# Scan adds and segment sums put on GpSimd, first state reloads issued from GpSimd's queue, half of Wo loaded behind the first attention outputs

## The chip, the cores and the metric

The kernel runs on one core of one Trainium2 chip. The metric is the device time of one execution in microseconds (us). A time below is the median of several executions, with the lowest and highest in brackets.

The engines are called PE (TensorE, the matmuls), VectorE (DVE in the profile), ScalarE (ACT), GpSimd (POOL) and SyncE (SP, which here only issues DMAs). Each works through its own instructions in order.

## The reference, cut to what matters

Two layers read inputs of 2048 x 1024 each, and their results are put side by side.

```python
# A: a state space layer, 1024 complex states
h = Lam_bar[None, :] * h + Bu[:, t, :]                     # for each of 2048 steps
y = 2.0 * einsum('blp,dp->bld', hseq, Cmat).real + x * Dskip
# B: attention over 64 segments of 32 tokens with 8 memory rows, 32 heads of 128
h = concatenate([mem, xs], axis=1)                          # for each segment
q, k, v = h @ Wq, h @ Wk, h @ Wv
o = softmax(mask(q @ k.T * scale)) @ v                      # by head
o = einsum('bhte,hed->btd', o, Wo); mem = o[:, :8]; outs.append(o[:, 8:])
```

## The kernel before

The kernel runs through four stages.

1. For each of 8 blocks of 128 states and each of 4 blocks of 512 steps, PE makes 16 products of 128x512 for A (L225) and, between them, 32 products for B's values (L364). VectorE turns A's products, runs two scans, and turns them back. The states go to DRAM.
2. The states are reloaded and multiplied by C (L284). Products of B's mean with Wo (L404 below, "the Wo products") stand between.
3. Attention.
4. Its outputs are reloaded and multiplied by Wo (L597).

```python
# stage 1, one block of states (pc) and one block of steps (tb)
V.tensor_tensor(wr[:], ur[:], c_, ALU.mult)      # ur, ui lie in PSUM, c_ and s_ in SBUF
V.tensor_tensor(ta[:], ui[:], s_, ALU.mult)
V.tensor_tensor(wr[:], wr[:], ta[:], ALU.add)                  # L231
V.tensor_tensor(wi[:], ui[:], c_, ALU.mult)
V.tensor_tensor(ta[:], ur[:], s_, ALU.mult)
V.tensor_tensor(wi[:], wi[:], ta[:], ALU.subtract)             # L234
V.tensor_tensor_scan(wr[:], rb, wr[:], ..., ALU.mult, ALU.add) # L237
V.tensor_tensor_scan(wi[:], rb, wi[:], ..., ALU.mult, ALU.add) # L238
...                                               # 2 casts on ScalarE, 6 bf16 operations on VectorE
k.SP.dma_start(self.hs[tb][:, pc, :, :], h[:])                 # L258, store of the states

# B's transposed input, 5 loads within the first block of states; each is followed by its sums
k.SP.dma_start_transpose(self.xe[:, :, c:c + n], self.x[0][t:t + n, :])
k.V.tensor_reduce(self.xsum[...], self.xe[...].rearrange("p c (s n) -> p c s n", n=SEG), AX.X, ALU.add)

# stage 2
for tb in range(NB):
    for q in range(4):                            # 0.5 MB each
        k.SP.dma_start(hl[q][:], self.hs[tb][:, 2 * q:2 * q + 2, :, :])
    if dB is None:
        k.SP.dma_start(dB[:], self.Dskip...)      # L271
    for tt in range(4):
        k.SP.dma_start(xn[:], self.x[0][t0:t0 + 128, :])       # L275
        G.tensor_tensor(xd[:], xn[:], dB[:], ALU.mult)         # L277, the skip product
        for half in range(2):
            ...                                   # 16 matmuls into py, one of two PSUM tiles (L284)
            V.tensor_tensor(ot[:, hs], py[:], xd[:, hs], ALU.add)  # L286, frees py
```

When the sums of all five loads are there, VectorE makes the segment means `b_xbar`. PE multiplies them by Wv once for each block of states (L381) and transposes the result (L386). The attention masks and a few constants are built on GpSimd, out of about 60 small operations which the scheduler places in the first block of states.

## Time and profile before

| what | value |
|---|---|
| time | 1345.31 us (1342.99 to 1346.76, 4 runs) |
| PE busy | 1288.2 of 1344.6 us in the profiled run |
| VectorE / GpSimd busy in 120 to 360 us | 209.6 / 0 of 240 us, with PE at 238.8 |
| waits of PE over 4 us | 8.3, 7.6, 7.1, 5.5, 4.8, 4.5 us |

The first view is the page's 40 slices of the span: each digit is the busy share of one slice in tenths, for PE and for GpSimd.

```profile
PE   6898999999979999999999999999999969999998
...
POOL 5000000000012221222222222222223220000000
```

PE is full but for the first slices and the slice near 1100 us (the 6 late in its row). A dip at 390 us hides in a slice of 7. GpSimd has nothing to do in stage 1 after the first slice. That is the spare time which the change wants to use.

The second view is the list of waits of PE: what it waited for, us in total, times, and the longest.

```profile
PE psP L597 <- DMA b_ol<-b_os_90: 8.3, 1, 8.3
PE psO L284 <- DMA a_hl_3523<-a_hs_70: 7.6, 1, 7.6
...
PE psR L386 <- ACT b_vst L62: 5.2, 2, 4.5
PE psP L364 <- DMA b_xe<-in_B_x_dram: 4.8, 1, 4.8
```

The first line is the tail of attention, the second the reload of the states, the third (4.5 of its 5.2 us) a transpose at 114 us, the fourth the fourth load of B's input at 47 us. (It is called "block 3" below, as the count starts at 0.)

In VectorE's timeline (start, duration, engine, line, operation), the first add of the second pair, and the scan that needs it:

```profile
36.93 0.68 DVE L231 TENSOR_TENSOR a_wr<-a_wr,a_ta 128x512 f32<-128x512 f32 x1
...
38.73 1.27 DVE L237 TENSOR_TENSOR_SCAN a_wr<-a_rr,a_nx,a_wr 128x512 f32<-128x512 f32 x1
```

The pair runs at 37 to 41 us, each add in 0.68 us. In SyncE's timeline, the load of B's block 3 is issued before the second store of states:

```profile
44.74 4.92 SPq L338 DMA_TRANSPOSE b_xe<-in_B_x_dram  x1
...
57.83 0.45 SPq L258 DMA_DIRECT2D a_hs_71<-a_h  x1
```

SyncE's timeline at the reload shows 1 MB of Wv issued just before the first states:

```profile
383.05 0.54 SPq L351 DMA_DIRECT2D b_wv<-in_B_Wv_dram  x1
383.64 0.61 SPq L268 DMA_DIRECT2D a_hl_3523<-a_hs_70  x1
...
385.94 0.43 SPq L271 DMA_DIRECT2D a_dB<-in_A_Dskip_dram  x1
```

### The profile page before, as it was taken

What the parts mean: (1) busy time and instruction counts of PE and PEld (TensorE: products, weight loads), DVE (VectorE), ACT (ScalarE), POOL (GpSimd) and SP (SyncE); (2) the same over time, 40 slices, a digit from 0 to 9 for tenths busy, and PEclk for the clock granted to TensorE, in tenths of its full rate; (3) what the DMA queues carried; (4) which work ended last, traced back from release to release, by engine and by line L of the source; (5) the groups of instructions that cost most, each with busy time, mean ns of one, the idle gap of its engine ahead of it and who ended that gap; (6) DMA issues with size and microseconds to landing.
All of it is one profiled execution on the core that took longest, in us unless ns stands there. A gap on an engine that the chain in (4) does not pass through costs nothing. (4 is left out here: it accounts for less than half of the span.)

```text
span 1344.6 us, 19373 instructions
## 1 busy us (share of the span) xinstructions
PE 1288.2 (96%) x7456; PEld 658.4 (49%) x7522; DVE 672.0 (50%) x1490; ACT 434.3 (32%) x1145; POOL 206.0 (15%) x283
## 2 busy tenths in 40 slices
PE   6898999999979999999999999999999969999998
PEld 2343444444434445555555555555555534444443
DVE  6899988888831223455555555555555520001000
ACT  2234333443310000454544545445545530001000
POOL 5000000000012221222222222222223220000000
PEclk9899999999989999999999999999999979999999
DMA  9983423332369726434343433333333082403000
GB/s 225 251 196 118 112 90 104 118 117 71 102 231 326 252 67 203 112 97 130 97 130 97 130 97 114 107 89 90 89 95 89 11 268 85 141 16 125 17 16 26
DMA packets 218873, 163.12 MB, mean 121 GB/s; under 512 B 74944, under 2 KB 198448, under 8 KB 218776
## 3 DMA queue, kind: packets, MB, share of 16 engines
q1 hardware_dynamic: 218200, 161.33, 41.4%
q8 instruction: 61, 1.00, 0.3%
q0 software_dynamic: 512, 0.47, 0.1%
q14 instruction: 36, 0.29, 0.1%
q10 hardware_dynamic: 64, 0.02, 0.0%
HBM read 95.72 MB, written 49.30 MB: 108 GB/s over the span
## 5 line engine op out<-in xcount | busy, mean ns | idle before, releaser
L364 PE MATMUL psP<-b_wv,b_xe 128*128 128x512 bf16 x996 | 226.6, 381 | 7.1 <-DMA b_xe<-in_B_x_dram 4.8
L509 ACT ACTIVATE b_e<-psS 99x396 bf16<-99x396 f32 x176 | 88.2, 501 | 338.9 <-PE psS L506 336.5
L512 POOL TENSOR_TENSOR b_m<-b_e,maskB 99x396 bf16<-99x396 bf16 x160 | 139.4, 871 | 355.3 <-ACT b_e L509 355.3
L532 DVE TENSOR_TENSOR b_ot<-psO,b_r 128x384 bf16<-128x384 f32 x176 | 98.1, 558 | 189.4 <-ACT b_r L526 168.7
L364 PEld LDWEIGHTS <-b_xe 128*128 128x128 bf16 x1024 | 100.4, 98 | 127.6 <-DMA b_xe<-in_B_x_dram 6.4
L597 PEld LDWEIGHTS <-b_ol 128*128 128x128 bf16 x896 | 88.0, 98 | 115.5 <-DMA b_ol<-b_os_90 8.1
L62 ACT ACTIVATE b_vst<-psP 128x512 bf16<-128x512 f32 x128 | 75.0, 588 | 142.2 <-PE psP L364 126.6
L64 DVE CAST b_ost<-psP 128x512 bf16<-128x512 f32 x16 | 11.1, 692 | 202.8 <-PE psP L597 202.8
L597 PE MATMUL psP<-t_4361,b_ol 128*128 128x512 bf16 x438 | 101.0, 385 | 8.7 <-DMA b_ol<-b_os_90 8.3
L597 PE MATMUL psP<-wo_11767,b_ol 128*128 128x512 bf16 x438 | 98.8, 379 | 0.5
L526 ACT ACTIVATE b_r<-b_ln 128x396 f32<-128x396 f32 x176 | 94.0, 534 | 5.4
L525 ACT ACTIVATE b_ln<-psR 128x396 f32<-128x396 f32 x176 | 86.9, 494 | 0.0
L62 ACT ACTIVATE b_ost<-psP 128x512 bf16<-128x512 f32 x16 | 9.6, 597 | 220.7 <-PE psP L597 207.4
L286 DVE TENSOR_TENSOR a_ot<-psO,a_xd 128x512 bf16<-128x512 f32 x32 | 22.1, 692 | 109.5 <-PE psO L284 89.4
L64 DVE CAST b_k_4366<-psP 128x480 bf16<-128x480 f32 (+2 forms) x96 | 48.8, 529 | 32.7 <-PE psP L482 32.2
L530 PE MATMUL psO<-b_m,b_v 99*128 99x99 bf16 x704 | 61.4, 209 | 1.8 <-DMA b_v<-b_vx_74 1.8
L521 PE MATMUL psR<-b_m,ones 99*128 99x396 bf16 x176 | 59.0, 335 | 3.1 <-POOL b_m L512 2.3
L277 POOL TENSOR_TENSOR a_xd<-a_xn_3533,a_dB 128x1024 f32<-128x1024 bf16 x1 | 2.1, 2117 | 374.2 <-DMA a_xn_3533<-in_A_x_dram 374.2
L64 DVE CAST b_k_4374<-psP 128x480 bf16<-128x480 f32 (+2 forms) x96 | 48.7, 528 | 21.2 <-PE psP L482 21.2
L530 PEld LDWEIGHTS <-b_v 99*128 99x128 bf16 x704 | 50.5, 98 | 15.3 <-DMA b_v<-b_vx_74 2.1
L64 DVE CAST b_q_4362<-psP 128x480 bf16<-128x480 f32 (+2 forms) x96 | 48.7, 528 | 17.5 <-PE psP L482 17.5
L64 DVE CAST b_q_4370<-psP 128x480 bf16<-128x480 f32 (+2 forms) x96 | 48.6, 528 | 12.5 <-PE psP L482 12.5
(719 smaller groups left out, 1986.1 us busy)
## 6 DMA issues: line engine op xcount, KB each, us to landing
b_wv<-in_B_Wv_dram SPq DMA_DIRECT2D x16, 1024.0 KB
b_wog<-in_B_Wo_dram SPq DMA_DIRECT2D x8, 1024.0 KB
out_dram<-a_ot SPq DMA_DIRECT2D x16, 256.0 KB
t_4361<-in_B_Wo_dram SPq DMA_DIRECT2D x1, 4096.0 KB
wo_11767<-in_B_Wo_dram SPq DMA_DIRECT2D x1, 4096.0 KB
b_ol<-b_os_90 SPq DMA_DIRECT2D x4, 1024.0 KB
b_ol<-b_os_91 SPq DMA_DIRECT2D x4, 1024.0 KB
b_ol<-b_os_92 SPq DMA_DIRECT2D x4, 1024.0 KB
```

The lines of the kernel that those rows point to most:

```text
L62: self.S.activation(out, in_, ACT.Copy)
L64: self.V.tensor_copy(out, in_)
L286: V.tensor_tensor(ot[:, hs], py[:], xd[:, hs], ALU.add)
L364: k.PE.matmul(p[:], self.xe[:, c, t * 128:(t + 1) * 128], w[:, c, :], start=(c == 0), stop=(c == KC - 1))
L509: k.S.activation(e[:], s[0:GW], ACT.Exp, scale=float(E) ** -0.5, accum_out=self.accE[0:GW, i:i + 1])
L512: k.G.tensor_tensor(m[:], e[:], mask[0:GW, :, :].unsqueeze(2).to_broadcast([GW, 2, 2, GW]), ALU.mult)
L521: PE.matmul(sm[:, 0:W4], k.ones[0:GW, :], mf, start=True, stop=True)
L525: k.S.activation(ln[:], sm[:, 0:W4], ACT.Ln)
L526: k.S.activation(r[:].rearrange("p a b q -> p (a b q)"), ln[:], ACT.Exp, scale=-1.0, accum_out=self.accR[:, i:i + 1])
L530: PE.matmul(o[:, gg, hh, :], vt[:, 2 * u + gg, hh * 128:(hh + 1) * 128], m[:, gg, hh, :], start=True, stop=True)
L532: V.tensor_tensor(ot[:, :, 2 * u * GX:(2 * u + 2) * GX].rearrange("p h (g n) -> p g h n", n=GX), o[:, :, :, 0:GX], r[:, :, :, 0:GX], ALU.mult)
L597: PE.matmul(p[:], lhs, self.wo[half][:, h, :], start=(h == 0), stop=(h == H - 1))
```

## The change

The intent is to relieve VectorE in stage 1 of 64 adds and of the sums, by using the idle GpSimd, and to take two loads out of SyncE's queue or forward in it.

```diff
-        ta = self.wp.tile([128, TB], FP32, name="a_ta", bufs=1)
+        ta = self.wp.tile(..., name="a_ta"); tb_ = self.wp.tile(..., name="a_ta")
-        V.tensor_tensor(wr[:], wr[:], ta[:], ALU.add)
+        k.G.tensor_tensor(wr[:], wr[:], ta[:], ALU.add)
-        V.tensor_tensor(wi[:], wi[:], ta[:], ALU.subtract)
+        k.G.tensor_tensor(wi[:], wi[:], tb_[:], ALU.subtract)
...
-                k.SP.dma_start(hl[q][:], self.hs[tb][:, 2 * q:2 * q + 2, :, :])
+                (k.G if tb == 0 else k.SP).dma_start(hl[q][:], self.hs[tb][:, 2 * q:2 * q + 2, :, :])
...
-            k.V.tensor_reduce(self.xsum[...], self.xe[...], AX.X, ALU.add)
+            ns = n // SEG
+            for h in range(0, KC, 4):
+                src = self.xe[:, h:h + 4, c:c + n].rearrange("p c (s n) -> p c s n", n=SEG)
+                a = self.xtmp.tile([128, 4, 15, SEG // 2], FP32, name="b_xa", bufs=1)
+                k.G.tensor_tensor(a[:, :, 0:ns, :], src[:, :, :, 0:16], src[:, :, :, 16:32], ALU.add)
+                for m in (8, 4, 2):
+                    k.G.tensor_tensor(a[:, :, 0:ns, 0:m], a[:, :, 0:ns, 0:m], a[:, :, 0:ns, m:2 * m], ALU.add)
+                k.G.tensor_tensor(self.xsum[...], a[:, :, 0:ns, 0], a[:, :, 0:ns, 1], ALU.add)
...
-            k.SP.dma_start(wo1, b.Wo[:, :, 512:D])
+            tc.keep_in_program_order(k.SP.dma_start(wo1, b.Wo[:, :, 512:D]))
```

The last edit keeps the load of Wo's second half (4 MB) from being moved ahead of the first loads of attention outputs, `b_ol`. From L339 on, the changed kernel's lines are 7 higher (L364 is L371, L381 is L388, L386 is L393).

More of the change, by code (lines that the diff above doesn't have):

```diff
@@ L227, in stage1 @@
         wr = self.wp.tile([128, TB], FP32, name="a_wr"); wi = self.wp.tile([128, TB], FP32, name="a_wi")
-        ta = self.wp.tile([128, TB], FP32, name="a_ta", bufs=1)
+        ta = self.wp.tile([128, TB], FP32, name="a_ta"); tb_ = self.wp.tile([128, TB], FP32, name="a_ta")
         V.tensor_tensor(wr[:], ur[:], c_, ALU.mult)
         V.tensor_tensor(ta[:], ui[:], s_, ALU.mult)
-        V.tensor_tensor(wr[:], wr[:], ta[:], ALU.add)
+        k.G.tensor_tensor(wr[:], wr[:], ta[:], ALU.add)
         V.tensor_tensor(wi[:], ui[:], c_, ALU.mult)
-        V.tensor_tensor(ta[:], ur[:], s_, ALU.mult)
-        V.tensor_tensor(wi[:], wi[:], ta[:], ALU.subtract)
+        V.tensor_tensor(tb_[:], ur[:], s_, ALU.mult)
+        k.G.tensor_tensor(wi[:], wi[:], tb_[:], ALU.subtract)
         rb = self.rr[:, pc:pc + 1].to_broadcast([128, TB])
@@ L338, in load_x @@
             k.SP.dma_start_transpose(self.xe[:, :, c:c + n], self.x[0][t:t + n, :])
-            k.V.tensor_reduce(self.xsum[:, :, t // SEG:(t + n) // SEG], self.xe[:, :, c:c + n].rearrange("p c (s n) -> p c s n", n=SEG), AX.X, ALU.add)
+            ns = n // SEG
[5 more added lines that the diff above has]
+                    k.G.tensor_tensor(a[:, :, 0:ns, 0:m], a[:, :, 0:ns, 0:m], a[:, :, 0:ns, m:2 * m], ALU.add)
+                k.G.tensor_tensor(self.xsum[:, h:h + 4, t // SEG:(t + n) // SEG], a[:, :, 0:ns, 0], a[:, :, 0:ns, 1], ALU.add)
     def fin_xbar(self, tmp):
@@ L765, in kernel_main @@
         with pool("p1", "right") as p1:
-            a.tab = a.tmp = a.wp = a.btp = p1
+            a.tab = a.tmp = a.wp = a.btp = b.xtmp = p1
             wv = b.load_wv(0)
```

## The prediction

> **What bounds it.** TensorE: by the page it is busy 1288 of 1345 us, and by the windows 39.8 of every 40 us from 120 to 360 us. A change pays only where TensorE stands still. The waits of PE and its timeline show where: 7.1 + 5.5 us before the first inputs; 4.8 us at 47 us (third block of B's transposed x); 4.5 us at 114 us (a transpose behind a ScalarE copy, ScalarE itself behind a late VectorE); 7.6 us at 382 us (first reload of states); 8.3 us at 1092 us (first attention outputs, queued behind 4 MB of Wo). After the long ones the granted clock is 0.5 for some us.
>
> **What moves.** 64 adds of 0.68 us and the segment sums (4 x 4.15 + 2 x 0.68 us) leave VectorE: 61 us of 672. In the middle that is worth nothing: VectorE is 88% busy there, TensorE 99%. GpSimd gets them. Its product of 128x396 took 871 ns (2.2 ns an element), that of 1024 2.12 us; the Trainium skill (GPSIMD Engine Reference, 3.1) has the same 2.2 ns (4497 ns for 2048). So I estimate 1.1 us for one add of 512 and, for half a block of sums (960+480+240+120+60 elements), 4.1 us: 37 us of sums in all.
>
> **Start: a loss.** GpSimd's program order puts the sums of block 1 (two halves) and all masks (about 10 us) before the second pair of scan adds. From the landing of block 0 (17.2 us) that gives the adds at about 48 to 52 us, where VectorE did them at 37 to 40. VectorE (scan) and ScalarE wait in order behind them. SyncE's order also changes: the store of the second states now stands before the transpose that loads x's block 3. I estimate that store at 58 us, block 3 at about 66 us (before: 52). TensorE's wait there grows from 4.8 to about 18 us in sum (part of it may show as a wait for b_vst copies). The segment mean is then ready at about 81 us. Net against before: +14 us.
>
> **Middle: a gain.** With VectorE unloaded the 4.5 us wait at 114 us should vanish, with the slow clock after it: -5.5.
>
> **State reload: a gain.** The loads leave SyncE's queue, where they stood behind the last stores and 1 MB of Wv (issued 383.6, landed 390.2). On GpSimd they wait only for the last read of xT (about 373) and GpSimd's last subtraction (about 377 on the old time scale). The 7.6 us wait should fall below 2 us, and the clock stay up: -9.
>
> **Wo's second half: a gain.** b_ol now goes first; 1 MB takes about 3.2 us, so it lands before the attention tail ends at 1092; Wo half 2 (needed 30 us later) follows. -8.5.
>
> **Sum:** 1345.9 + 14 - 5.5 - 9 - 8.5 = 1337; I say 1338, range 1324 to 1353. Faster by over 2%: 0.05; within 2%: 0.91; slower: 0.04.
>
> **What would show it.** Waits of PE: b_ol gone, a_hl under 2 us, the wait at 114 us gone, and more idle before 85 us than now (25 us up to the segment-mean product's transposes, then about 39). GpSimd nearly full from 17 to 80 us, its add of 512 at 1.1 us; VectorE idle on GpSimd at 37 to 48 us; 120 to 360 us still at 39.8 of 40.
>
> **What would make it wrong.** GpSimd slower than 2.2 ns an element on short strided rows or beside a busy VectorE (shared SBUF port): the start loses more, and over 2 us an add could make VectorE pace the middle. Or VectorE/SyncE not being held as I think: the start loses nothing, and 1325 results. Software-made descriptors for the reloads may also be slower than I assume.

## More of the kernel before

The group of the first scan, from the list of groups (count, then busy us and mean ns):

```profile
L237 DVE TENSOR_TENSOR_SCAN a_wr<-a_rr,a_nx,a_wr 128x512 f32<-128x512 f32 x24 | 30.6, 1275 | 0.0
```

## The result, and the profile after

The changed kernel took 1363.66 us (1361.47 to 1364.17, 4 runs), against 1345.31 us before. The ratio is 1.0135, with a 95% interval of 1.0116 to 1.0154. It is 18 us slower. Ratios in this document are the mean time of one kernel's runs over that of the other's runs of the same rounds, so they are not quite the ratios of the medians quoted.

PE's list of waits after:

```profile
PE psP L371 <- ACT b_vst L62: 17.1, 5, 14.0
PE psR L388 <- DVE b_xbar L354: 8.8, 1, 8.8
PE psP L371 <- DMA b_xe<-in_B_x_dram: 7.9, 1, 7.9
...
PE psO L284 <- DVE a_ot L286: 6.5, 1, 6.5
```

The waits for `b_ol`, `a_hl` and the transpose at 114 us are gone, 20.4 us in sum (8.3 + 7.6 + 4.5). In their place stand 17.1 us for the copies `b_vst`, 8.8 us for the means (0.8 before), 7.9 us for block 3, and 6.5 us for `a_ot`. A ledger by landmarks of PE shows where the time went:

| landmark of PE | before, us | after, us | shift |
|---|---|---|---|
| goes on with B's block 3 | 52.14 | 75.99 | +23.9 |
| first product with the means | 79.32 | 98.50 | +19.2 |
| second product with the means | 111.20 | 143.78 | +32.6 |
| its transposes | 118.59 | 146.60 | +28.0 |
| first product of stage 2 | 390.24 | 408.95 | +18.7 |
| first Wo product of stage 2 | 402.95 | 427.66 | +24.7 |
| last product of attention | 1091.80 | 1117.01 | +25.2 |
| first product of the last stage | 1100.60 | 1117.77 | +17.2 |

The two lines of the first product with the means, before and after:

```profile
79.32 1.91 PE L381 MATMUL psR<-b_wv,b_xbar 128*64 128x512 bf16 x8 [0.84 <-DVE b_xbar L347]
...
98.50 3.48 PE L388 MATMUL psR<-b_wv,b_xbar 128*64 128x512 bf16 x8 [8.76 <-DVE b_xbar L354]
```

This landmark is not at the same place in PE's order. Counted by weight loads, 248 matmuls of A and of B's values stand before it in the kernel before, and 192 in the change: with the sums on GpSimd the scheduler put the product 56 matmuls earlier. It is so in every run below that has the sums on GpSimd; where the adds moved and the sums did not, it stands behind 231. The second product has 384 before it in every run, and its transposes follow closely, so these two can be compared.

The start lost 32.6 us, read at the second product. Up to there PE was idle for 48.0 us instead of 20.2, and the same matmuls took 95.7 us instead of 91.0, at a mean granted clock of 0.88 instead of 0.97. So 4.8 us of the loss are slower matmuls, and 27.8 are waits. The middle gave back 6.2 of it (4.6 at the transposes, 1.6 more up to the end of stage 1). The reload gave 7.7 and lost 6.0 of that within 19 us. The end gave 8.0.

**The start.** All engines' timeline around the second pair of scan adds shows the chain:

```profile
53.45 1.26 POOL L231 TENSOR_TENSOR a_wr<-a_wr,a_ta 128x512 f32<-128x512 f32 x1
54.67 1.99 POOL L343 TENSOR_TENSOR b_xa<-b_xe 128x960 f32<-128x960 bf16 x1
54.74 2.99 DVE L237 TENSOR_TENSOR_SCAN a_wr<-a_rr,a_nx,a_wr 128x512 f32<-128x512 f32 x1 [13.61 <-POOL a_wr L231]
56.61 2.18 POOL L234 TENSOR_TENSOR a_wi<-a_wi,a_ta 128x512 f32<-128x512 f32 x1
...
57.77 0.63 ACT L248 ACTIVATE a_gr<-a_wr 128x512 bf16<-128x512 f32 x1 [18.25 <-DVE a_wr L237]
...
58.93 1.44 PE L371 MATMUL psP<-b_wv,b_xe 128*128 128x512 bf16 x3 [14.02 <-ACT b_vst L62]
```

VectorE waited 13.6 us for the first add, ScalarE 18.3 us for the scan, and PE 14.0 us for the copy that stands behind ScalarE's cast. GpSimd had been busy all that time, with sums and masks. After the add it put the next sum (L343) first, and only then the second add, as its order says. SyncE then reached its store late, and block 3 was issued behind it:

```profile
67.83 0.33 SPq L258 DMA_DIRECT2D a_hs_71<-a_h  x1
...
68.69 4.86 SPq L338 DMA_TRANSPOSE b_xe<-in_B_x_dram  x1
```

Block 3 was issued at 68.7 us where it had been 44.7.

**The middle.** The scan that now runs beside a GpSimd add nearly doubled:

```profile
L237 DVE TENSOR_TENSOR_SCAN a_wr<-a_rr,a_nx,a_wr 128x512 f32<-128x512 f32 x24 | 54.2, 2259 | 26.3 <-POOL a_wr L231 26.3
```

The all-engine timeline shows one case of it, and the reload's place in GpSimd's order:

```profile
401.35 1.26 POOL L234 TENSOR_TENSOR a_wi<-a_wi,a_ta 128x512 f32<-128x512 f32 x1
401.42 2.27 DVE L237 TENSOR_TENSOR_SCAN a_wr<-a_rr,a_nx,a_wr 128x512 f32<-128x512 f32 x1 [0.25 <-POOL a_wr L231]
402.55 0.59 POOL L268 DMA_DIRECT2D a_hl_3621<-a_hs_70  x1
```

GpSimd's add (L234) was there first, at 401.35. The scan started to count at 401.42, and took 2.27 us where it takes 1.27 alone. If it stood still until the add ended at 402.61, 1.08 us remain for it. The Trainium skill says this of the two engines' shared port pair ("SBUF — State Buffer", section "SBUF: two separate sides"): whichever starts first gets it for the whole instruction, and "the other fully blocks". This trace agrees. The multiplication with one input in PSUM ran from 400.49 beside the other add in 0.68 us, so it was not held. Of the 43 us of adds that left VectorE (64 x 0.68), (2259 - 1275) ns x 24 + (2135 - 1215) ns x 8 = 31 us came back as longer scans. PE did 238.84 of 240 us between 120 and 360 us in both kernels, so neither mattered there.

**The reload.** The timeline after the last transposes of stage 1:

```profile
409.99 0.59 SPq L358 DMA_DIRECT2D b_wv<-in_B_Wv_dram  x1
...
410.67 0.59 SPq L271 DMA_DIRECT2D a_dB<-in_A_Dskip_dram  x1
...
419.63 2.11 POOL L277 TENSOR_TENSOR a_xd<-a_xn_3631,a_dB 128x1024 f32<-128x1024 bf16 x1 [14.90 <-DMA a_xn_3631<-in_A_x_dram]
...
422.51 1.86 PE L284 MATMUL psO<-t_105,a_hl_3621 128*128 128x512 bf16 x4 [6.49 <-DVE a_ot L286]
```

The states were there, but the third output tile of stage 2 needs a free PSUM tile. VectorE frees it with `a_ot`, which needs the skip product `a_xd` (L277). Its loads, Dskip and x, are still on SyncE, now issued behind 1 MB of Wv.

### The profile page after: what moved, and what is told of

Same layout as the page of the kernel before. It is cut to its first block, busy times and chain, and to the rows that moved or that the text cites. A ratio compares the mean times of both kernels' runs of the same rounds, so it can differ in the third digit from the quotient of the medians.

```text
span 1362.5 us, 19503 instructions
## 1 busy us (share of the span) xinstructions
PE 1291.1 (95%) x7457; PEld 658.7 (48%) x7522; DVE 663.3 (49%) x1420; ACT 429.6 (32%) x1145; POOL 340.3 (25%) x411
## 5 line engine op out<-in xcount | busy, mean ns | idle before, releaser
L371 PE MATMUL psP<-b_wv,b_xe 128*128 128x512 bf16 x1015 | 229.7, 384 | 25.5 <-ACT b_vst L62 17.1
L371 PEld LDWEIGHTS <-b_xe 128*128 128x128 bf16 x1024 | 100.9, 99 | 150.1 <-issue 23.4
L62 ACT ACTIVATE b_vst<-psP 128x512 bf16<-128x512 f32 x128 | 69.5, 588 | 117.5 <-PE psP L371 77.6
L231 POOL TENSOR_TENSOR a_wr<-a_wr,a_ta 128x512 f32<-128x512 f32 x32 | 40.6, 1268 | 235.4 <-DVE a_ta L230 235.4
L237 DVE TENSOR_TENSOR_SCAN a_wr<-a_rr,a_nx,a_wr 128x512 f32<-128x512 f32 x24 | 54.2, 2259 | 26.3 <-POOL a_wr L231 26.3
L64 DVE CAST b_k_4464<-psP 128x480 bf16<-128x480 f32 (+2 forms) x96 | 48.8, 529 | 32.7 <-PE psP L489 32.2
L64 DVE CAST b_k_4472<-psP 128x480 bf16<-128x480 f32 (+2 forms) x96 | 48.6, 528 | 21.3 <-PE psP L489 21.3
L64 DVE CAST b_q_4460<-psP 128x480 bf16<-128x480 f32 (+2 forms) x96 | 48.6, 528 | 17.5 <-PE psP L489 17.5
```

Of the source, the lines that this page charges most:

```text
L62: self.S.activation(out, in_, ACT.Copy)
L64: self.V.tensor_copy(out, in_)
L237: V.tensor_tensor_scan(wr[:], rb, wr[:], 0.0 if ini is None else ini[:, 0:1], ALU.mult, ALU.add)
L371: k.PE.matmul(p[:], self.xe[:, c, t * 128:(t + 1) * 128], w[:, c, :], start=(c == 0), stop=(c == KC - 1))
```

## The experiments

Thirteen kernels ran. Q stands for GpSimd's queue (what stands before what, and for how long), P for the two engines holding each other off. Runs of one batch share their runs of before.

| run | time, us | ratio to before, 95% interval |
|---|---|---|
| the change | 1363.66 | 1.0135 (1.0116 to 1.0154) |
| e1_sums_back | 1333.93 (1333.73 to 1336.18) | 0.9915 (0.9893 to 0.9938) |
| e2_adds_back | 1356.46 (1354.64 to 1357.64) | 1.0073 (1.0050 to 1.0096) |
| e3_reload_only | 1343.24 (1341.75 to 1344.59) | 0.9978 (0.9960 to 0.9995) |
| e4_wo_only | 1336.96 (1335.25 to 1339.31) | 0.9933 (0.9915 to 0.9951) |
| e5_masks_early | 1358.18 (1356.47 to 1358.76) | 1.0086 (1.0065 to 1.0107) |
| e6_skip_early | 1337.25 (1335.89 to 1339.18) | 0.9933 (0.9910 to 0.9956) |
| e7_best_adds | 1335.41 (1333.25 to 1336.13) | 0.9926 (0.9909 to 0.9942) |
| e8_best_noadds | 1329.46 (1325.76 to 1331.50) | 0.9878 (0.9858 to 0.9899) |
| e9_port_arms | 1335.25, one run, state unknown | |
| e10_copies | 1346.49 (1344.23 to 1346.84) | 1.0006 (0.9986 to 1.0027) |
| e11_masks_copies | 1338.89 (1337.71 to 1340.18) | 0.9953 (0.9932 to 0.9973) |
| e12_last_on_v | 1327.51 (1326.59 to 1328.23) | 0.9867 (0.9850 to 0.9883) |
| e13_one_input | 1366.56 (1365.50 to 1367.34) | 1.0161 (1.0144 to 1.0178) |

Before took 1346.71 us in the batch of e1 to e4, 1346.07 in that of e5, e6 and e9, 1344.35 in that of e7, e8, e10 and e11, and 1344.73 in the last.

### Parts undone and parts alone

**The change with the sums back on VectorE.**

```diff
-                k.G.tensor_tensor(a[...], ...)      # the five adds for each half
+            k.V.tensor_reduce(self.xsum[...], self.xe[...], AX.X, ALU.add)
```

> The change with the segment sums back on VectorE (one tensor_reduce per block); scan adds, reloads and Wo order as in the change. Theory Q (queue): the start lost 32 us because the scan adds stand behind the sums in GpSimd's in-order queue, and VectorE, ScalarE and SyncE's stores stand behind the adds. Without the sums the start loss is gone (mean product ready at 80 us or earlier, block 3 of x landed by 54 us) and the time is 1330 to 1337 us. Rival P (port): GpSimd and VectorE keep each other off whenever both have two-input work, so adds on GpSimd are of no use to VectorE; then the first scan still takes about 2.27 us (1.27 before), and the start still loses 5 to 10 us: 1340 to 1346 us.

Measured: 1333.93 us, 30 us less than the change. PE went on with block 3 at 49.80 us, and the first product with the means came at 77.11. The scans stayed long (mean 2103 ns), and that cost nothing. PE reached the second product's transposes at 118.35 us, as before (118.59). So the sums on GpSimd are what slows the change, alone or together with the adds.

**The change with the scan adds back on VectorE.**

```diff
-        k.G.tensor_tensor(wr[:], wr[:], ta[:], ALU.add)
+        V.tensor_tensor(wr[:], wr[:], ta[:], ALU.add)      # and the subtraction likewise
```

> The change with the scan adds back on VectorE; the sums stay on GpSimd. Theory Q: nothing that VectorE needs early waits for GpSimd now except the segment mean, which GpSimd should have at about 75 to 85 us; block 3 of x lands by 55 us; time 1335 to 1342 us. Rival P: the sums stretch VectorE's two-input instructions from 17 to 85 us (single ones of 2 us and more), VectorE falls behind as it did before or worse, and the start loses over 10 us: 1347 us or more.

Measured: 1356.46 us, the rival's side. PE's waits:

```profile
PE psR L388 <- DVE b_xbar L354: 16.9, 1, 16.9
```

With no adds in the queue, the means still came late: GpSimd's sums and masks ran almost without a gap from 17.2 to 88.7 us, and the product with the means came at 90.79 instead of 79.32. The transposes of the second product came at 139.18, so 20.6 of the change's 28.0 us at this landmark are the sums' (and the masks' between them), and 7.4 the adds' behind them. The masks were longer here (16.3 us against 11.9), with VectorE busy for 43.4 of the 46 us from 22 to 68 us (32.4 in the change). Part of the 16.9 us may come from PE's order, in which the product stands 56 matmuls earlier than before; no run has the sums on GpSimd with PE's old order, so how much stays open. My theory that the place of the adds was the main thing falls: the larger part is the work that GpSimd must do before the means.

**Before with the reload issued from GpSimd.**

```diff
-                k.SP.dma_start(hl[q][:], self.hs[tb][...])
+                (k.G if tb == 0 else k.SP).dma_start(hl[q][:], self.hs[tb][...])
```

> The kernel before with the first state reloads issued from GpSimd and nothing else. My theory: the 7.6 us wait for a_hl goes, but the third output tile of stage 2 then waits about 6 us for the products x*D, whose inputs still stand behind 1 MB of Wv on SyncE's queue; the time falls by only 1 to 3 us: 1342 to 1344.5. Rival: the 6.5 us wait in the changed kernel comes from GpSimd or VectorE being behind there; alone, the reload then gains 8 to 10 us: 1335 to 1337.

Measured: 1343.24 us. The `a_hl` wait was gone and an `a_ot` wait of 4.5 us stood in its place, as expected.

**Before with Wo's half behind the first attention outputs.**

```diff
-            k.SP.dma_start(wo1, b.Wo[:, :, 512:D])
+            tc.keep_in_program_order(k.SP.dma_start(wo1, b.Wo[:, :, 512:D]))
```

> The kernel before with the second half of Wo kept behind the first attention outputs and nothing else. Expected: the 8.3 us wait for b_ol falls to under 0.5 us and the time by 7 to 8.5 us: 1337 to 1338.5. Rival: the loads moved forward collide with the last loads of v or weights in the attention stage and give part of it back there: gain under 5 us.

Measured: 1336.96 us, 0.67% under before, that is 9 us. The `b_ol` wait was gone. This part of the change was read right.

**Before with the reload and the loads for the skip product on GpSimd.**

```diff
-                k.SP.dma_start(hl[q][:], self.hs[tb][...])
+                (k.G if tb == 0 else k.SP).dma_start(hl[q][:], self.hs[tb][...])
-                k.SP.dma_start(dB[:], self.Dskip...)
+                k.G.dma_start(dB[:], self.Dskip...)
-                k.SP.dma_start(xn[:], self.x[0][t0:t0 + 128, :])
+                (k.G if t0 < 256 else k.SP).dma_start(xn[:], self.x[0][t0:t0 + 128, :])
```

> Before, with the first reload issued from GpSimd (as in the run of the reload alone) and, right behind it, also the load of Dskip and the first two tiles of x that the skip product a_xd needs. Theory: the reload alone gained only 3 us since the wait moved to a_ot behind a_xd behind these loads, which stood in SyncE's queue behind 1 MB of Wv. With them out of it the a_ot wait (4.5 us with the reload alone) is under 1 us, the clock stays up, and the time is 1335 to 1339 (7 to 9 under before). Rival: 1 MB of Wv, or the first Wo tile, occupies the DMA engines, so the loads land late whoever issues them; then the wait stays above 3 us and the time is 1341 to 1344.

Measured: 1337.25 us, and no `a_ot` wait. GpSimd's timeline has the reloads from 371.9 us, Dskip and x right behind them (373.4 and 374.0), and the skip product at 381.6 us (387.8 in the run of the reload alone):

```profile
371.88 1.57 POOL L268 DMA_DIRECT2D a_hl<-a_hs  x3 [34.77 <-PE psO L225]
...
381.60 4.75 POOL L277 TENSOR_TENSOR a_xd<-a_xn,a_dB 128x1024 f32<-128x1024 bf16 x2 [6.56 <-DMA a_dB<-in_A_Dskip_dram]
```

0.67% of 1346 us are 9 us, three times what the reload alone gave. The gain that I had put on the reload is there; it takes three loads more.

### What the queue costs, and what the port

**The change with the masks built early,** in GpSimd's idle first 17 us.

```diff
-                    if tb == 0 and pc == 1:
-                        masks(k)
-                        check_consts(k)
+            masks(k)                # ahead of a.tables(0), before the loop
+            check_consts(k)
```

> The change, with the attention masks and check constants (about 12 us of small GpSimd work that stood between the sums of blocks 1 and 2) built in GpSimd's idle first 17 us. Theory Q (the start loss is GpSimd's in-order queue: what stands before the second pair of scan adds and before the last sum): the second pair of adds moves from 53.5 to about 42 us, x's block 3 resumes TensorE near 65 instead of 76 us, the segment-mean product starts near 87 instead of 98 us, and the time falls by 8 to 11 us against the change: 1351 to 1356. Theory P (VectorE and GpSimd hold each other off; the sums and adds are stretched whatever stands between them): the sums stretch all the same and the time stays at 1359 or more.

Measured: 1358.18 us, 5.5 us less than the change and between the two theories. The timeline around the second pair:

```profile
46.66 1.38 POOL L231 TENSOR_TENSOR a_wr<-a_wr,a_ta 128x512 f32<-128x512 f32 x1 [0.53 <-DVE a_ta L230]
...
48.00 1.98 POOL L343 TENSOR_TENSOR b_xa<-b_xe 128x960 f32<-128x960 bf16 x1
48.07 2.99 DVE L237 TENSOR_TENSOR_SCAN a_wr<-a_rr,a_nx,a_wr 128x512 f32<-128x512 f32 x1
```

VectorE did not wait for the queue here. GpSimd waited 0.53 us for it, as VectorE itself was late: it was busy 41.6 of the 46 us from 22 to 68 us (32.4 in the change). Its scan took 2.99 us beside the sum L343, which had come 0.07 us before. So what the queue no longer took, the hold-off took in part, and neither theory has the number alone.

**A probe of the scan,** sums on VectorE, five arms by block of states in one kernel.

```diff
+        if pc in (2, 3, 4): V adds wr        else: GpSimd adds wr
+        if pc in (2, 3, 4, 5): V subtracts wi  else: GpSimd subtracts wi
+        if pc == 3: k.G.tensor_copy(jk[:], tb_[:])
+        if pc == 4: k.G.tensor_scalar(jk[:], tb_[:], 1.0, None, ALU.mult)
```

> A probe, sums on VectorE, of what a GpSimd operation beside the first scan does to the scan. Five arms by state block: blocks 0, 1, 6, 7 both adds on GpSimd as in the change; block 2 both adds on VectorE, nothing beside the scan; block 3 as 2, with a GpSimd tensor_copy of 128x512 f32 (one input, result unused) released as the scan starts; block 4 the same with a GpSimd tensor_scalar (one input); block 5 only the first add on GpSimd, done before the scan. Theory P1 (two SBUF inputs on both engines exclude each other): scan means 2.1 to 2.3 us with both adds on GpSimd, 1.25 to 1.35 in blocks 2 and 5, and 1.25 to 1.4 in blocks 3 and 4. Rival P2 (any GpSimd operation on SBUF excludes it): blocks 3 and 4 also near 2 us. The time itself should be within 3 us of the run with the sums on VectorE (1333.9), as TensorE bounds the middle.

The groups of the first scan by arm (L259 both adds on GpSimd, L257 only the first, L251 none, L253 none but the copy released as the scan starts; L255, with the multiplication, also had 1274 ns):

```profile
L259 DVE TENSOR_TENSOR_SCAN a_wr<-a_rr,a_nx,a_wr 128x512 f32<-128x512 f32 x12 | 24.2, 2019 | 2.3 <-POOL a_wr L237 2.3
...
L257 DVE TENSOR_TENSOR_SCAN a_wr<-a_rr,a_nx,a_wr 128x512 f32<-128x512 f32 x3 | 3.8, 1283 | 0.8 <-POOL a_wr L237 0.8
...
L251 DVE TENSOR_TENSOR_SCAN a_wr<-a_rr,a_nx,a_wr 128x512 f32<-128x512 f32 x3 | 3.8, 1274 | 0.0
...
L253 DVE TENSOR_TENSOR_SCAN a_wr<-a_rr,a_nx,a_wr 128x512 f32<-128x512 f32 x3 | 3.8, 1274 | 0.0
```

The scan is long only where an add that started before it runs beside it: 2019 ns on average (just under the 2.1 us expected) against 1274 to 1283. This does not clear the one-input operations, as the timeline shows (a case of L253):

```profile
198.59 1.27 DVE L253 TENSOR_TENSOR_SCAN a_wr<-a_rr,a_nx,a_wr 128x512 f32<-128x512 f32 x1
...
198.73 1.54 POOL L247 COPY a_jk<-a_ta 128x512 f32<-128x512 f32 x1 [8.82 <-DVE a_ta L239]
...
199.78 1.03 DVE L241 TENSOR_TENSOR a_wi<-a_wi,a_ta 128x512 f32<-128x512 f32 x1
```

Here the scan was first, by 0.14 us, and the copy was the one that grew: 1.54 us, where a copy of 480 elements took 0.59 us in another run (below). VectorE's next operation (L241) then took 1.03 us instead of 0.68. So my reading of this probe by "one input or two" was badly made. Which came first decided, as the skill has it.

**The sums' adds replaced by copies,** a wrong result: each `tensor_tensor` of the sums becomes a `tensor_copy` of one input. The flag that would start the kernel's slow general path is set to 0. The order on every engine is that of the change. (The comparison with the reference passed all the same, so this result does not hang on the means within its tolerance.)

```diff
-                    k.G.tensor_tensor(a[..., 0:m], a[..., 0:m], a[..., m:2 * m], ALU.add)
+                    k.G.tensor_copy(a[..., 0:m], a[..., m:2 * m])
```

> The change with every add of the segment sums on GpSimd replaced by a copy of one of its inputs (same tiles, same sizes, same instruction order on every engine), and the check's flag set to 0, so the result is wrong on purpose. It takes the second SBUF input away and leaves GpSimd's queue as it is. Theory Q (queue order and length): VectorE still waits 12 to 14 us for the second pair of scan adds, and the time stays within 4 us of the change: 1360 to 1367. Theory P (hold-off): VectorE's stretched operations at the start go back to their own length, GpSimd's too, and the time falls by more than 8 us, under 1356. If copies turn out much shorter than adds the queue shrinks too, and only the durations in the trace decide.

> Both at once: masks built in GpSimd's idle first 17 us, and copies for the sums' adds (wrong on purpose). With the masks early alone (1358.2) VectorE no longer waited for the queue (0.5 us before the second pair) but was busy 45.8 of the 46 us from 22 to 68 us with operations that I estimate at 28.5 us by their own shortest durations in the trace of before. If that stretch (P) is what kept the time at 1358, it falls to 1340 to 1349 here, with VectorE busy under 36 us in that stretch. If the sums' mere length on GpSimd (mean ready late) is what counts, it stays at 1353 or more.

Measured: 1346.49 us with the copies, 17 us less than the change, and 1338.89 us with copies and early masks. But a copy took half an add's time (0.98 us instead of 1.99 for 960 elements, 0.59 instead of 1.20 for 480), so queue and port shrank together. These two runs show only that less work on GpSimd undoes most of the loss: PE reached the second product's transposes at 127.97 and 124.01 us, against 146.60 in the change and 118.59 before. With copies and early masks VectorE was busy for 39.6 of the 46 us, not under 36, and the time fell below the range given for it, so the test as I had set it decides nothing. (The 45.8 us in the expectation are a sum of timeline rows, which overlap a little; the busy view had 41.6. Summed in the same way this run has 43.6.)

**One input, but as long as an add,** again wrong: multiplications by 1.0 in place of the sums' adds, the order on every engine again that of the change.

```diff
-                    k.G.tensor_tensor(a[..., 0:m], a[..., 0:m], a[..., m:2 * m], ALU.add)
+                    k.G.tensor_scalar(a[..., 0:m], a[..., m:2 * m], 1.0, None, ALU.mult)
```

> The change with every add of the segment sums on GpSimd replaced by a multiplication by 1.0 of one of its inputs (one SBUF input instead of two; same tiles, sizes and instruction order on every engine; flag set to 0; wrong on purpose). The copies were half as long as the adds, so they shortened the queue too; in the probe this operation took about 1.4 us of its own for 512 elements, as long as an add. Theory Q' (what counts is how long GpSimd is occupied, whatever its number of inputs): the time stays at 1357 to 1367. Theory P' (the second SBUF input is what holds VectorE off and is held off itself): the time falls to 1344 to 1353, as with the copies, with the second pair of adds at about 45 us though the sums take as long. If the durations turn out shorter than the adds', the run says no more than the copies did.

Measured: 1366.56 us; the time did not fall. The all-engine timeline at the second pair:

```profile
57.91 2.61 POOL L343 TENSOR_SCALAR b_xa<-b_xe 128x960 f32<-128x960 bf16 x1
57.98 1.99 DVE L237 TENSOR_TENSOR_SCAN a_wr<-a_rr,a_nx,a_wr 128x512 f32<-128x512 f32 x1 [18.41 <-POOL a_wr L231]
```

VectorE was busy only 22.5 of the 46 us from 22 to 68 us, and it waited 18.4 us for the queue; PE waited 17.8 us at a stretch for the copies behind it, and 12.1 for the means. VectorE was less stretched than in the change: the rows of its timeline in these 46 us sum to 26.0 us, where the shortest durations of the same operations in the trace of before sum to about 22.1; in the change they are 37.2 and 23.9. It was not free of it: the scan shown took 1.99 us. It ended 0.55 us before the multiplication that had started first, so it did not wait for the whole of it: here the trace does not agree with the skill's sentence, as it does for the adds. The multiplications were even longer than adds (2.61 us for 960 elements, 1.41 for 480), so the queue was a little longer than the change's. Still, the loss is whole with VectorE stretched by about 4 us instead of 13. With the order on every engine fixed, how long GpSimd is occupied before the adds and the means is what sets the start.

The start in one table. GpSimd's busy us are summed from its timeline, operations that started between 17 and 98 us (rows overlap by some hundredths of a us). The landmarks are PE's. Ahead of the first one the runs with sums on GpSimd have 192 matmuls, before has 248 and e1_sums_back 231:

| run | sums | masks | adds | first product with the means | transposes of the second |
|---|---|---|---|---|---|
| before | 0 | not counted | 0 | 79.32 | 118.59 |
| the change | 51.6 | 11.9 | 11.0 | 98.50 | 146.60 |
| e1_sums_back | 0 | not counted | not counted | 77.11 | 118.35 |
| e2_adds_back | 51.1 | 16.3 | 0 | 90.79 | 139.18 |
| e5_masks_early | 49.9 | 0 | 11.4 | 93.18 | 141.12 |
| e10_copies | 34.1 | 11.9 | 13.6 | 81.44 | 127.97 |
| e11_masks_copies | 34.1 | 0 | 15.5 | 75.84 | 124.01 |
| e13_one_input | 54.0 | 10.9 | 10.1 | 101.98 | 149.81 |

The copies' 34.1 us still hold some waiting for VectorE: three copies at 53.8 us took 4.55 us, and 1.39 alone.

### A version that beats both

> The version that should beat both: scan adds on GpSimd as in the change, segment sums left on VectorE, reload from GpSimd with Dskip and the first two x tiles right behind it, Wo's half behind the first attention outputs. From the single runs: 1333.9 with the sums back, less about 6 for the a_ot wait: 1326 to 1330.

> The same with the scan adds left on VectorE too: nothing but the three moves of loads. Gains of the single runs add: 1346 - 9 (reload and skip loads) - 9 (Wo) = 1328, range 1326 to 1331. Theory: moving the scan adds is worth nothing or up to 3 us (the 4.5 us wait at 114 us stays here), so this is 0 to 3 us slower than the run with the adds moved; a rival that holds the scan adds worth their 43 us of VectorE time, even in part, would have it 5 us or more slower.

The first is the change with the sums on VectorE and the skip product's loads early. The second leaves the adds on VectorE too, and is before with nothing but the three moves of loads:

```diff
+ e8: before, with the edits of e6_skip_early and e4_wo_only
+ e7: e8, and the scan adds on GpSimd as in the change
```

Measured: 1335.41 and 1329.46 us. The second was as expected. The first was 5 us over the top of its range, and 6 us slower than the second, where I had expected it to be up to 3 us faster. Its timeline at the reload:

```profile
374.46 2.18 POOL L268 DMA_DIRECT2D a_hl<-a_hs  x4
...
388.15 0.93 SPq L400 DMA_DIRECT2D b_wog<-in_B_Wo_dram  x2
...
394.18 1.87 PE L404 MATMUL psS<-b_wog,b_gx 128*73 128x512 bf16 x4 [6.24 <-DMA b_wog<-in_B_Wo_dram]
```

The reloads were issued at 374.5 us, right behind the last scan add (373.3, 1.27 us). (In the second they went out at 370.3.) Then the first Wo tile was issued late, at 388.2 us, since its issue waits for the last stores to land, and PE waited 6.2 us for it. My explanation was that 2 MB of reloads, sent 4 us later, ran into those stores. The test: in the first version, put the adds of the last block of states alone back on VectorE.

```diff
-        k.G.tensor_tensor(wr[:], wr[:], ta[:], ALU.add)
+        (V if pc == PC - 1 else k.G).tensor_tensor(wr[:], wr[:], ta[:], ALU.add)   # wi likewise
```

> The version with the scan adds on GpSimd, all loads early and the sums on VectorE (1335.4), with the adds of the last state block alone put back on VectorE. Theory R: there the four reloads stood behind the last adds on GpSimd (issued at 374.5 us where they were issued at 370.3 us with no adds), their 2 MB ran into the last stores, Wv and Wo, and the first Wo tile came 6 us late. Then the reloads are issued near 370 us, the 6.2 us wait for b_wog is under 1 us, and the time is 1326 to 1331. Rival S: the adds on GpSimd slow the stage in some other way (start, stretched scans); then it stays at 1334 to 1336.

```profile
371.48 2.17 POOL L268 DMA_DIRECT2D a_hl<-a_hs  x4 [40.65 <-PE psO L225]
...
385.00 0.93 SPq L400 DMA_DIRECT2D b_wog<-in_B_Wo_dram  x2
...
392.33 1.89 PE L404 MATMUL psS<-b_wog,b_gx 128*73 128x512 bf16 x8 [0.91 <-DMA b_wog<-in_B_Wo_dram]
```

Measured: 1327.51 us. The reloads went out at 371.5, Wo's tile at 385.0, and the longest wait for it was 0.9 us. So the last adds on GpSimd, with the reload behind them, are what had cost the 8 us. The last store was issued at 379.64 us in the first version and at 379.66 here, so the longer scans had not delayed it; Wo's issue waited for it to land for 6.3 us there and 3.1 here. PE's order differs too: there 32 products of the states stand before the first Wo product, here 48, so a part of the 6.2 us may be PE's having less to do before it. How much was not tested, and that the stores landed late because of the reloads' traffic was not measured by itself. This version and the second one can't be told apart (their intervals overlap), so 56 adds on GpSimd are worth nothing measurable even where they do no harm.

## Why the prediction was wrong

The time predicted was 1338 us in a range of 1324 to 1353. It was 1363.66. Point by point:

- **"What bounds it": right.** PE bounds the middle in both kernels, 238.84 of 240 us.
- **"Start: a loss", +14 us: right in mechanism, wrong in size.** It was +32.6: 27.8 us of waits, and 4.8 of slower matmuls that the +14 (39 - 25 us of idle time) had no term for. The step that failed is the sum of GpSimd's work before the means. By my estimates it was 37 + 10 us, and 8 adds of 1.1, about 56 us. It measured 76.6 (sums 51.6, masks 11.9, adds 11.0, DMA issues 2.1) of the 81.3 us from 17.2 to 98.5. An estimate from the trace splits the sums: a half-block's five adds with little beside them take 1.99 + 1.20 + 0.70 + 0.40 + 0.30 = 4.59 us, not 4.1, and eight of these with four small parts of about 1.58 us make 43. The other 8.6 us are adds of the sums that took longer beside VectorE's work (one of 480 elements took 4.34 us). So the second pair of adds came at 53.5 and 56.6 us (predicted 48 to 52), the store behind them at 67.8 (58), block 3 at 76.0 (66), and the means at 98.5 (81). e1_sums_back and e2_adds_back show that the sums carry most of it, and e13_one_input that their length does it with VectorE much less stretched. What PE's changed order (the product with the means 56 matmuls earlier) adds to the wait for the means stays open. I had named the shared port under "what would make it wrong", but gave it no microseconds.
- **"Middle: a gain", -5.5 us: right in size, but the mechanism is not shown.** It was -6.2. The wait at 114 us is just as gone in e2_adds_back (no wait where there were 4.5 us), with the adds on VectorE and PE 20.6 us later. With the adds moved and the sums back (e1_sums_back, e7_best_adds, e12_last_on_v) it fell to between 0.8 and 1.6 us, but PE then reached these transposes at 118.3 to 118.5 us, no earlier than before (118.59). So an unloaded VectorE is one reading, and PE's late arrival, which gave VectorE time to catch up, is another; the agreement in size may be luck. The adds also came back as longer scans, which I had not predicted, but PE did not see it.
- **"State reload: a gain", -9 us: wrong.** It was -1.7. The `a_hl` wait went away as predicted. The step that failed is that nothing else would be waited for: the skip product's loads stood in the same place of SyncE's queue and became the next wait, 6.5 us. e6_skip_early got the whole gain by moving these too. e7_best_adds and e12_last_on_v show a second thing that I had missed: on GpSimd the reload stands behind the last scan adds.
- **"Wo's second half: a gain", -8.5 us: right.** It was -8.0 in the ledger and about -9 alone.

The two wrong sizes make 18.6 + 7.3 = 25.9 us of the 25.7 by which the prediction missed. "GpSimd nearly full from 17 to 80 us" held. "Its add of 512 at 1.1 us" did not: it took 1.27.

## What to carry to other kernels

An idle engine is not free room when others wait for it in order: add up all the work that it will have ahead of each result that someone needs early, with its durations measured at the sizes used, and put what is needed first in front. When a load is moved off a queue, ask which load or product will be the next to be waited for, and move that too; the three moves of loads alone gave 1.2%. Work taken from an engine that is not the bottleneck bought nothing here, however many microseconds it was.

## What the Trainium skill lacked or had wrong

- "GPSIMD Engine Reference", section 3.1, has 4497 ns for an add of 2048 fp32 elements, 2.2 ns an element; it names a dispatch cost for each instruction on GpSimd but gives no figure for it. Here an add of 512 took 1.27 us (2.5 ns an element) and one of 60 took about 0.3 us (5 ns). Small strided adds need that term; my estimate of the sums without it was 6 us short (43 against 37).
- The same page, section 4.1 (Engine selection), calls one-input operations on GpSimd "roughly line-rate". The copy was (0.98 us for 960 elements). The multiplication by a constant, also with one input, took 2.61 us, longer than the two-input add (1.99).
- "SBUF — State Buffer" says that the engine which comes first keeps the port pair for the whole instruction. The scans agree beside an add (2.27 us, 1.27 alone), but not beside a one-input multiplication of 960 elements (e13_one_input): that started first, at 57.91 us, and took 2.61, and the scan ended at 59.97, 0.55 us before it. The page also does not say what several GpSimd instructions in a row do. A 128x8 operation of VectorE (L173) took 5.76 us at 23.45 us in the changed kernel, while GpSimd ran four two-input adds back to back, and ended with the fourth (29.2 us).
- "DMA: Bandwidth & Descriptors", section "Issuing engines are not separate DMA queues", says that issuing from several engines only saves the time of the issue. That leaves out the place in the engine's order: issued from GpSimd, and not behind SyncE's last stores and Wv, the reload and the skip product's loads gained 9 us (e6_skip_early); behind the last scan adds on GpSimd they lost 8 again (e7_best_adds against e12_last_on_v, where PE's order differed too).
